# Another way to load and turn the queries and keys of the first head pair

## The chip, the cores and the metric

The kernel runs on one core of a Trainium2 chip. A core has TensorE (matmuls; PE in the profile, PEld for its weight loads), VectorE (DVE), ScalarE (ACT), GpSimd (POOL) and SyncE (SP, which here only issues DMAs), and 16 DMA engines that all queues share. The metric is the device time of one execution in microseconds; the times given are the median of several runs and the time of the one execution that was profiled.

## What is computed

Attention with a threshold, and a feed-forward layer with an ELU behind it:

```python
scores = scale * np.matmul(q, k.transpose(0, 1, 3, 2))      # scale = 1/8
thresh = np.max(scores, axis=-1, keepdims=True) - tau
scores = np.where(scores >= thresh, scores, -1000000000.0)
scores = scores - np.max(scores, axis=-1, keepdims=True)
attn = np.exp(scores)
attn = attn / (np.sum(attn, axis=-1, keepdims=True) + 1e-09)
x = np.matmul(attn, v)             # (8, 8, 576, 64) -> x of (4608, 512)
h = x @ w_in                       # (512, 2048)
g = np.where(h > 0.0, h, np.exp(np.minimum(h, 0.0)) - 1.0)
out = g @ w_out                    # (2048, 512)
```

q, k and v have batch 8, 8 heads, 576 rows and 64 columns, in float32. tau is 0.02, and the kernel reads it at run time.

## The kernel before

**Pairs and steps.** Two heads are worked on together, one on partitions 0 to 63 and one on 64 to 127, so there are 32 pairs, four to a batch entry. The 576 query rows of a pair make five steps: four of 128 rows (i = 0 to 3) and a tail (i = 4) of 64 rows from each head, joined through the tile `qd`. A step consists of the scores of 128 queries against 576 keys for each head (`scores`, L269, matmuls at L283), their maximum on VectorE (`max_of`, L319), the exponential on ScalarE (`exp_of`, L328), the threshold on GpSimd (`bound_of`, L323), the mask with the row sum on VectorE (`mask_of`, L338), the sum and its reciprocal (L347), the normalization on GpSimd (`normalize`, L313), and the turning of the weights on TensorE (`turn_parts`, L365), whose results ScalarE copies out of PSUM (L370). Two steps later follow the products with v (`values`, L479).

**Order of the work.** The first four pairs run in the loop at L780 inside `tc.manual_schedule()`: instructions stand on each engine in the order in which the program names them, and each engine works through its own queue. Later stages (from L870 on) weave the feed-forward layer of earlier batch entries into the attention of later pairs, with an order made by a planner with written-down shifts (`MOVED`); the change doesn't touch them. In the loop, step n works on its scores while the weights of step n-1 are normalized and turned. Idle transposes of the identity (`idle`, L767, and `spare` in `room`, L372) fill TensorE's time: 28 before the first scores, 16 in the first step, then 9 and 11 in each further step of the first pair, and 6 and 8 in later pairs.

**Buffers.** Scores lie in PSUM tiles `sc` from a pool of three (L99). The first step takes two of them. The second step's head 0 takes the third, and its head 1 takes the one that the first step's head 0 frees when its mask has been made. The raw tiles `qm` and `km` (pool `raw`, one buffer for each name) hold a pair's q and k until they are turned.

**How q and k come in.** `load` (L195) fetches q and k of a pair as pieces of 32 numbers: four DMAs for each, one for a head and a half of its 64 columns, each to 32 partitions. The layout is such that VectorE's turn of 32x32 blocks (`prep_q` L219, `prep_k` L228) gives qT and kT, with the 64 columns of each head on partitions. For the first pair SP issues q, then tau, and ACT issues k (L760 to L762); then SP issues v of pair 0, and q, k and v of pair 1. `copy_k` (L240) puts the last 64 keys of head 1 in front of its keys as well, and `copy_q` (L233) fills `qd`; both are on GpSimd. The scores of head 1 read what `copy_k` writes.

**The scale.** In all pairs but the first, GpSimd multiplies qT by `keep` (`scale_q`, L224); `keep` is 1/8 where tau is not negative, and 0 otherwise. In the first pair q is not scaled. There the exponential takes the scale from `keep`, and its bias, the negated maximum, is first multiplied by `keep` on ScalarE (`nb`, L333); the threshold uses `ntau0`, which is `ntau` times 8 (L117). `read_tau` (L111) derives these from tau on VectorE.

Of the kernel before, what the change touches and what calls it, by code (L numbers as in the profile page):

```python
# [10 lines left out]
FP32 = mybir.dt.float32  # L11
U32 = mybir.dt.uint32
I32 = mybir.dt.int32
AF = mybir.ActivationFunctionType
ALU = mybir.AluOpType
# [34 lines left out]
def kernel(  # L50
# [10 lines left out]
    nc = tc.nc  # L61
    PSUM = bass.MemoryType.PSUM
    P = 128
    B, H, S, D = q.shape
# [3 lines left out]
    TAIL = S - MAIN  # L68
    HALF = S // 2
# [7 lines left out]
    SCALE = 1.0 / 8.0  # L77
# [3 lines left out]
    const = ctx.enter_context(tc.tile_pool(name="const", bufs=1))  # L81
    raw = ctx.enter_context(tc.tile_pool(name="raw", bufs=1))
    qkp = ctx.enter_context(tc.tile_pool(name="qkp", bufs=2))
# [9 lines left out]
    wstage = early.enter_context(tc.tile_pool(name="wstage", bufs=2))  # L93
    wpool = [wstage]
    banks = ExitStack()
    psum = {"t": banks.enter_context(tc.tile_pool(name="ps_t", bufs=2, space=PSUM))}
# [4 lines left out]
    ident = wstage.tile([P, P], FP32, name="ident", bufs=1)  # L101
# [4 lines left out]


    tau_sb = const.tile([P, 1], FP32, name="tau_sb")
    pos, keep, far, ntau, ntau0 = (const.tile([P, 1], FP32, name=x) for x in ("pos", "keep", "far", "ntau", "ntau0"))

    def read_tau():  # L111
        nc.vector.tensor_scalar(pos, tau_sb, 0.0, None, ALU.is_ge)
        nc.vector.tensor_scalar(keep, pos, SCALE, None, ALU.mult)
        nc.vector.tensor_scalar(far, pos, -FAR, FAR, ALU.mult, ALU.add)
        nc.vector.tensor_tensor(ntau, tau_sb, far, ALU.max)
        nc.vector.tensor_scalar(ntau, ntau, -1.0, None, ALU.mult)
        nc.vector.tensor_scalar(ntau0, ntau, 1.0 / SCALE, None, ALU.mult)  # L117

    w_in_sb = const.tile([P, KJ, DF], FP32, name="w_in_sb")
    w_out_sb = const.tile([P, NFT, DM], FP32, name="w_out_sb")  # L120
# [4 lines left out]
    qds = [const.tile([P, P], FP32, name=f"qd{i}") for i in range(NQD)]  # L125
# [66 lines left out]
    raws, pairs = {}, {}  # L192


    def load(pr, parts=("qm", "km", "v"), shared=False, queue=nc.sync):  # L195
        b, j = divmod(pr, NPAIR)
        tiles = raws.setdefault(pr, {})
        for name, src in (("qm", q), ("km", k)):
            if name not in parts:
                continue  # L200
            m = tiles[name] = raw.tile([P, S // T, T], FP32, name="qm" if shared else name)
            for i in range(2):
                for d in range(2):
                    r = (2 * i + d) * T
                    queue.dma_start(
                        m[r : r + T],
                        src[b, 2 * j + i].rearrange("(j t) d -> t j d", t=T)[:, :, d * T : (d + 1) * T],
                    )
        if "v" not in parts:
            return  # L210
        vm = tiles["vm"] = raw.tile([P, 2, NC, D], FP32, name="vm", bufs=2)
        vd = tiles["vd"] = vds[pr % NVD]
        for i in range(2):
            vh = v[b, 2 * j + i]
            nc.sync.dma_start(vm[:, i], vh[:MAIN].rearrange("(c p) d -> p c d", p=P))
            r = slice(i * TAIL, (i + 1) * TAIL)
            nc.sync.dma_start(vd[r, r], vh[MAIN:])

    def prep_q(pr):  # L219
        qT = qkp.tile([P, S], FP32, name="qT")  # L220
        nc.vector.transpose(qT, raws[pr]["qm"].rearrange("p j d -> p (j d)"))
        pairs[pr] = [qT, None, qds[pr % NQD]]
# [5 lines left out]
    def prep_k(pr):  # L228
        kT = pairs[pr][1] = qkp.tile([P, TAIL + S], FP32, name="kT")
        nc.vector.transpose(kT[:, TAIL:], raws[pr]["km"].rearrange("p j d -> p (j d)"))  # L230
# [9 lines left out]
    def copy_k(pr):  # L240
        kT = pairs[pr][1]
        nc.gpsimd.tensor_copy(kT[D:, :TAIL], kT[D:, S:])
# [16 lines left out]

    def vectors(pr):  # L260
        st = {x: small.tile([P, 2], FP32, name=x) for x in ("mx", "th", "su", "rs")}
        if not pr:
            st["nb"] = wstage.tile([P, 2], FP32, name="nb", bufs=4)
        step_no[0] += 1
        st["sm"] = totals[:, step_no[0] % 6]
        return st
# [55 lines left out]

    def bound_of(pr, i, h):  # L323
        st = open_steps[pr, i]
        nc.gpsimd.tensor_scalar(st["th"][:, h : h + 1], st["mx"][:, h : h + 1], -1.0, ntau if pr else ntau0, ALU.mult,
                                ALU.add)

    def exp_of(pr, i, h):  # L328
        st = open_steps[pr, i]
        bias = st["mx"][:, h : h + 1]  # L330
        if not pr:
            bias = st["nb"][:, h : h + 1]
            nc.scalar.mul(bias, st["mx"][:, h : h + 1], keep)  # L333
        e = e_slot()
        nc.scalar.activation(e, st[h][:, :, :HALF], AF.Exp, bias=bias, scale=1.0 if pr else keep)
        st[h] = st[h], e

    def mask_of(pr, i, h):  # L338
# [417 lines left out]

    with tc.manual_schedule():
        load(0, ("qm",))  # L760
        nc.sync.dma_start(tau_sb, tau.to_broadcast([P, 1]))
        load(0, ("km",), queue=nc.scalar)  # L762
        load(0, ("v",))
        load(1)


        def idle(n):  # L767
            rt = psum["t"].tile([P, NC, P], FP32, name="rt", tag="rt")
            for _ in range(n):
                transpose(rt[:, 0], ident)  # L770

        idle(28)
        prep_q(0)
        prep_k(0)
        read_tau()
        copy_k(0)
        copy_q(0)
        scores(0, 0, [0, 1])
        out_values = None
        for n in range(per_seq):  # L780
            pr, i = steps[n]
            hs = heads_of(i)
            x = progress[1]
            if n:
                normalize(*steps[n - 1], [0])
                turned = turn_parts(*steps[n - 1])
            max_of(pr, i, 0)
            exp_of(pr, i, 0)
            bound_of(pr, i, 0)

            first_scores = n > 2 and i in (2, NB - 1)
            if n and not first_scores:
                spare.append(6 if pr else 9)
                copies = turned[0]()
            if len(hs) == 2:
                max_of(pr, i, 1)
            if n and len(heads_of(steps[n - 1][1])) == 2:
                normalize(*steps[n - 1], [1])
            if len(hs) == 2:
                exp_of(pr, i, 1)  # L800
                bound_of(pr, i, 1)
            if out_values:
                out_values()
            if n and not first_scores:
                copies()

            if i == NB - 1 and n + 1 < per_seq:
                convert_top(x)
                convert_add(x)
                convert_abs(x)  # L810
                convert_rest(x + 1)
            elif i == 0 and n:
                convert_end(x)
                load_w()
            elif i == 1 and pr:
                convert_sign(x)
                convert_add(x)
            elif i in (2, 3):
                (prep_q if i == 2 else prep_k)(pr + 1)
                if i == 2:  # L820
                    scale_q(pr + 1)
                (copy_q if i == 2 else copy_k)(pr + 1)
            mask_of(pr, i, 0)
            if n and not first_scores:
                spare.append(8 if pr else 11)
                turned[1]()()
            elif not n:
                idle(16)
            if n + 1 < per_seq:
                scores(*steps[n + 1], heads_of(steps[n + 1][1]))  # L830
            if n:
                for part in turned[0 if first_scores else 2 :]:
                    part()()
            if len(hs) == 2:
                mask_of(pr, i, 1)
            reciprocal_of(pr, i, hs)
            out_values = None
            if n > 1 and steps[n - 2][1] in (1, NB - 1):
                out_values = values(steps[n - 2][0], 0 if steps[n - 2][1] == 1 else 1)
            if i == 0 and n:  # L840
                convert_shift(x + 1)
            elif i == 2 and pr:
                convert_end(x)
                load_w()
            if i == 1 and pr:
                convert_abs(x)
            if i == 2 and n + 3 < per_seq:
                convert_rest(progress[1])
            if i in (3, 4):
                load(pr + 2, ("qm",) if i == 3 else ("km",))  # L850
            if i == 3 and pr:
                load(pr + 1, ("v",))
            if n == 0:
                load_w()
                load_w()
        for h in heads_of(steps[per_seq - 1][1]):
            normalize(*steps[per_seq - 1], [h])
# [12 lines left out]
    with tc.manual_schedule():  # L870
# [3 lines left out]
        for n in range(per_seq, SWITCH):  # L874
            pr, i = step = steps[n]
# [167 lines left out]
    with tc.manual_schedule():  # L1043
        after = []
        make_out(1), make_out(0)
        for n in range(SWITCH, MIDDLE):
            pr, i = steps[n]
# [297 lines left out]
        queue = deque()  # L1345
# [213 lines left out]
```

## Time and profile before

| | |
|---|---|
| median of 3 runs | 1319.18 us (1317.34 to 1320.45) |
| profiled execution | 1320.34 us, of which the span of its instructions is 1318.6 us |
| TensorE busy | 1298.9 us (99%) |
| VectorE, ScalarE, GpSimd busy | 1012.1, 559.5 and 805.2 us |
| moved by DMA | 247.76 MB, 188 GB/s in the mean |
| first scores begin (L283) | 8.12 us |
| second step's idle transposes begin | 13.57 us |

Times within the profile are counted from the start of the span. A group or timeline line names the source line, the engine, the operation and "output<-input" with the program's names, then shapes and the count; brackets give how long the engine sat idle before and what released it. A matmul in float32 shows as two instructions. The idle transposes count as busy TensorE, so its 99% is not 99% of useful work.

### The profile page before, as it was taken

What the parts mean: (1) busy time and instruction counts of PE and PEld (TensorE: products, weight loads), DVE (VectorE), ACT (ScalarE), POOL (GpSimd) and SP (SyncE); (2) the same over time, 40 slices, a digit from 0 to 9 for tenths busy, and PEclk for the clock granted to TensorE, in tenths of its full rate; (3) what the DMA queues carried; (4) which work ended last, traced back from release to release, by engine and by line L of the source; (5) the groups of instructions that cost most, each with busy time, mean ns of one, the idle gap of its engine ahead of it and who ended that gap; (6) DMA issues with size and microseconds to landing.
All of it is one profiled execution on the core that took longest, in us unless ns stands there. A gap on an engine that the chain in (4) does not pass through costs nothing.

```text
span 1318.6 us, 22013 instructions
## 1 busy us (share of the span) xinstructions
PE 1298.9 (99%) x6980; PEld 1011.0 (77%) x6980; DVE 1012.1 (77%) x2195; ACT 559.5 (42%) x1219; POOL 805.2 (61%) x1186
## 2 busy tenths in 40 slices
PE   8999999999999999999999999999999999999998
PEld 7666756647778777777878777878777787888886
DVE  6877775988888988898898979897889882545534
ACT  5676664225353444444443535252526250422320
POOL 4657774768657665767475747584768463624533
PEclk9998999999999999999999999999999999999999
DMA  6255452788897989898889888989889775221221
GB/s 120 61 107 161 136 143 57 220 241 241 222 257 221 259 214 245 214 260 232 240 216 256 239 234 224 259 240 245 234 235 258 216 214 185 93 72 60 93 60 32
DMA packets 322595, 247.76 MB, mean 188 GB/s; under 512 B 208688, under 2 KB 284464, under 8 KB 322480
## 3 DMA queue, kind: packets, MB, share of 16 engines
q1 hardware_dynamic: 320112, 246.07, 68.6%
q8 instruction: 55, 0.90, 0.3%
q10 hardware_dynamic: 2368, 0.30, 0.2%
q14 instruction: 60, 0.49, 0.1%
HBM read 161.81 MB, written 84.48 MB: 187 GB/s over the span
## 4 chain that ended last, share of the span: by engine, by line
PE 93%; DVE 3%; DMA 1%; ACT 1%; issue 1%; SPq 1%; POOL 0%; ACTq 0%; DVEq 0%
PE f L1289 29%; PE f L1149 28%; PE sc L541 8%; PE sc L601 7%; PE rt L354 4%; PE sc L283 4%; PE f L652 4%; PE f L692 3%; PE pv L494 3%; PE sc L593 1%; PE sc L588 1%; DMA there<-x 1%; PE pv L489 1%; DVE x L428 1%; SPq L457 0%
## 5 line engine op out<-in xcount | busy, mean ns | idle before, releaser
L317 POOL TENSOR_SCALAR w<-w,rs 128x576 f32<-128x576 f32 x196 | 169.1, 871 | 85.6 <-DVE rs L351 75.5
L548 DVE TENSOR_REDUCE mx<-sc 128x1 f32<-128x576 f32 x207 | 148.3, 750 | 35.3 <-PE sc L541 32.4
L558 ACT ACTIVATE w<-sc,mx 128x576 f32<-128x576 f32 x115 | 83.0, 740 | 114.6 <-DVE mx L548 96.8
L1149 PE MATMUL f<-xt,sw 128*128 128x256 f32 x512 | 123.8, 384 | 0.8 <-ACT xt L611 0.5
L1149 PE MATMUL f<-xt,w_in_sb 128*128 128x256 f32 x512 | 122.3, 381 | 0.3 <-ACT w L1163 0.3
L554 POOL TENSOR_SCALAR th<-mx,ntau 128x2 f32<-128x2 f32 (+1 forms) x115 | 34.3, 298 | 137.8 <-DVE mx L548 137.8
L1149 PEld LDWEIGHTS f<-xt,w_in_sb 128*128 128x128 f32 x512 | 96.1, 190 | 16.0 <-ACT w L1163 3.2
L1149 PEld LDWEIGHTS f<-xt,sw 128*128 128x128 f32 x512 | 93.7, 190 | 18.2 <-ACT xt L611 0.9
L541 PE MATMUL sc<-kT,qT 64*128 64x512 f32 (+4 forms) x736 | 107.5, 423 | 0.0
L1149 PE MATMUL f<-x,w_in_sb 128*128 128x256 f32 x448 | 106.1, 379 | 1.4 <-ACT g L1210 1.4
L1289 PE MATMUL f<-w_out_sb,g 128*128 128x256 f32 x448 | 107.1, 382 | 0.0
L541 PEld LDWEIGHTS sc<-kT,qT 64*128 64x128 f32 x736 | 80.8, 186 | 34.2 <-issue 16.8
L1289 PE MATMUL f<-w_out_sb,s 128*128 128x256 f32 x448 | 107.0, 382 | 0.0
L1289 PE MATMUL f<-t,s 128*128 128x256 f32 x448 | 105.8, 379 | 0.0
L428 DVE STREAM_TRANSPOSE x<-w 128x512 f32<-128x512 f32 (+2 forms) x143 | 96.6, 709 | 10.6 <-POOL w L317 10.3
L562 DVE SCALAR_TENSOR_TENSOR w<-sc,th,w 128x576 f32<-128x576 f32 x115 | 89.8, 811 | 11.4 <-ACT w L558 9.2
L1236 POOL TENSOR_TENSOR s<-g 128x256 f32<-128x256 f32 x104 | 80.4, 779 | 29.4 <-PE f L1289 20.1
L1149 PEld LDWEIGHTS f<-x,w_in_sb 128*128 128x128 f32 x448 | 85.0, 190 | 13.4 <-ACT g L1210 1.8
L1289 PEld LDWEIGHTS f<-w_out_sb,g 128*128 128x128 f32 x448 | 84.1, 190 | 12.9 <-issue 0.7
L1289 PEld LDWEIGHTS f<-t,s 128*128 128x128 f32 x448 | 85.1, 190 | 11.6
L1289 PEld LDWEIGHTS f<-w_out_sb,s 128*128 128x128 f32 x448 | 84.2, 190 | 12.3
L317 POOL TENSOR_SCALAR e<-e,rs 128x576 f32<-128x576 f32 x92 | 68.5, 749 | 35.5 <-DVE rs L351 34.2
(193 smaller groups left out, 2858.7 us busy)
## 6 DMA issues: line engine op xcount, KB each, us to landing
there<-x SPq DMA_DIRECT2D x408, 144.0 KB, 3.7
wTb<-there SPq DMA_DIRECT2D x52, 576.0 KB, 6.5
wTa<-there SPq DMA_DIRECT2D x50, 576.0 KB, 4.9
sw<-win_sums SPq DMA_DIRECT2D x62, 384.0 KB, 4.2
t<-wout_sums SPq DMA_DIRECT2D x45, 512.0 KB, 5.7
qm<-in_q_dram SPq DMA_DIRECT2D x128, 72.0 KB, 4.5
vm<-in_v_dram SPq DMA_DIRECT2D x64, 128.0 KB, 3.2
wst<-in_moe_w_in_dram SPq DMA_DIRECT2D x16, 512.0 KB, 4.4
```

The lines of the kernel that those rows point to most:

```text
L283: nc.tensor.matmul(scs[h][:, a, :HALF], qs[r], kT[r, k0 : k0 + HALF], start=True, stop=True)
L317: nc.gpsimd.tensor_scalar(wv, wv, st["rs"][:, h : h + 1], 1.0, ALU.mult, ALU.mult)
L354: nc.tensor.matmul(dst, src, ident, is_transpose=True, skip_group_check=True)
L428: nc.vector.transpose(x[:, :, c0 : c0 + nc_], src.rearrange("p (c g n) -> p g c n", c=nc_, n=T))
L541: on_banks(nc.tensor.matmul(o, qT[r, i * P : (i + 1) * P], kT[r, k0 : k0 + n], start=True, stop=True, skip_group_check=True), o)
L548: on_banks(nc.vector.tensor_reduce(st["mx"][:, h : h + 1], st["sc", h], axis=AX.XY if i == NC else AX.X, op=ALU.max, negate=True), st["sc" ...
L558: on_banks(nc.scalar.activation(st["e", h], st["sc", h], AF.Exp, bias=st["mx"][:, h : h + 1]), st["sc", h])
L562: on_banks(nc.vector.scalar_tensor_tensor(st["e", h], st["sc", h], st["th"][:, h : h + 1], st["e", h], ALU.is_ge, ALU.mult, accum_out=st[" ...
L601: on_banks(nc.tensor.matmul(o, vm[:, h, c], parts[part][:, g0:g1, h * (NC + 1) + c], start=False, stop=(c == NC - 1), skip_group_check=Tru ...
L1149: nc.tensor.matmul(loc["banks"][place], left[:, j], right[:, j], start=(begins and j == 0), stop=(j == 1), skip_group_check=True)
L1236: engine.tensor_tensor(o, x, y, op)
L1289: nc.tensor.matmul(place(m), lhs, rhs, start=(begins and v == 0), stop=(v == RU - 1), skip_group_check=True)
```

## The change

For the first pair alone, q and k are loaded as rows of 64 numbers. 96 partitions hold six neighbouring rows each, for both heads; SP issues two DMAs for q, and ACT two for k. After 10 idle transposes instead of 28, TensorE turns six tiles of 96 rows for q and six for k into two of the three `sc` tiles in PSUM. VectorE reads q out, multiplied by `keep`, and ScalarE reads k out with a copy; both put every sixth row in its place, so their output steps by six numbers. `read_tau` now stands before these turns. Since the scores of the first pair now come out scaled, `exp_of` and `bound_of` are the same for all pairs: `nb`, its instruction on ScalarE, the scale operand of the exponential and `ntau0` are gone.

```diff
-    pos, keep, far, ntau, ntau0 = (const.tile([P, 1], FP32, name=x) for x in ("pos", "keep", "far", "ntau", "ntau0"))
+    pos, keep, far, ntau = (const.tile([P, 1], FP32, name=x) for x in ("pos", "keep", "far", "ntau"))
...
-        nc.vector.tensor_scalar(ntau0, ntau, 1.0 / SCALE, None, ALU.mult)
...
-        if not pr:
-            st["nb"] = wstage.tile([P, 2], FP32, name="nb", bufs=4)
...
-        nc.gpsimd.tensor_scalar(st["th"][:, h : h + 1], st["mx"][:, h : h + 1], -1.0, ntau if pr else ntau0, ALU.mult,
-                                ALU.add)
+        nc.gpsimd.tensor_scalar(st["th"][:, h : h + 1], st["mx"][:, h : h + 1], -1.0, ntau, ALU.mult, ALU.add)
...
-        bias = st["mx"][:, h : h + 1]
-        if not pr:
-            bias = st["nb"][:, h : h + 1]
-            nc.scalar.mul(bias, st["mx"][:, h : h + 1], keep)
         e = e_slot()
-        nc.scalar.activation(e, st[h][:, :, :HALF], AF.Exp, bias=bias, scale=1.0 if pr else keep)
+        nc.scalar.activation(e, st[h][:, :, :HALF], AF.Exp, bias=st["mx"][:, h : h + 1])
...
+    R = 96
     with tc.manual_schedule():
-        load(0, ("qm",))
+        rows = [wstage.tile([R, S // R, 2, D], FP32, name=x, bufs=1) for x in ("qn", "kn")]
+        for t, src, queue in zip(rows, (q, k), (nc.sync, nc.scalar)):
+            for h in range(2):
+                queue.dma_start(t[:, :, h], src[0, h].rearrange("(p r) d -> p r d", p=R))
         nc.sync.dma_start(tau_sb, tau.to_broadcast([P, 1]))
-        load(0, ("km",), queue=nc.scalar)
         load(0, ("v",))
         load(1)
...
-        idle(28)
-        prep_q(0)
-        prep_k(0)
+        idle(10)
         read_tau()
+        qT, kT = qkp.tile([P, S], FP32, name="qT"), qkp.tile([P, TAIL + S], FP32, name="kT")
+        pairs[0] = [qT, kT, qds[0]]
+        turned = []
+        for t in rows:
+            turned.append(psum["s"].tile([P, 2, 512], FP32, name="sc")[:, :, :HALF].rearrange("p a (r n) -> p a r n", n=R))
+            for x in range(S // R):
+                nc.tensor.matmul(turned[-1][:, x % 2, x // 2], t[:, x].rearrange("p h d -> p (h d)"), ident[:R, :R],
+                                 is_transpose=True, skip_group_check=True)
+        qo, ko = (t.rearrange("d (p r a) -> d a r p", r=S // R // 2, a=2) for t in (qT, kT[:, TAIL:]))
+        nc.vector.tensor_scalar(qo, turned[0], keep, None, ALU.mult)
+        nc.scalar.copy(ko, turned[1])
         copy_k(0)
         copy_q(0)
         scores(0, 0, [0, 1])
```

## The prediction

> **What bounds the kernel now.** I read the shares of busy time and of the chain of waits first, then that chain in order of time over the first 60 us, then windows over single stretches.
>
> ```profile
> PE 1298.9 (99%) x6980; PEld 1011.0 (77%) x6980; DVE 1012.1 (77%) x2195; ACT 559.5 (42%) x1219; POOL 805.2 (61%) x1186
> ...
> PE 93%; DVE 3%; DMA 1%; ACT 1%; issue 1%; SPq 1%; POOL 0%; ACTq 0%; DVEq 0%
> ```
>
> TensorE carries 93% of the chain, and the change leaves the work of pairs 1 to 31 as it is. What it can win or lose lies in the first pair. There the chain reads (start, duration, what):
>
> ```profile
> 2.34 4.41 DMA km<-in_k_dram
> ...
> 7.33 0.73 DVE kT L230
> 8.07 0.05 DVE pos L112
> 8.12 0.01 issue
> 8.12 1.62 PE sc L283 x8
> 9.74 1.90 PE rt L354 x16
> 11.63 0.68 PE sc L283 x2
> 12.31 0.12 issue
> 12.44 1.21 PE sc L283 x6
> 13.64 3.27 PE rt L354 x28
> 16.91 1.17 PE sc L283 x8
> ```
>
> Three places matter: the landing of k at 6.75; the first scores at 8.12; and the pause inside the second step's scores, six of whose eight instructions wait until 12.44. From 13.64 the chain is TensorE alone. That pause is explained by the order of time: the second slot for those scores is freed by the mask of the first step's head 0 (L344), which stands behind this series on ScalarE and VectorE:
>
> ```profile
> 10.19 0.29 ACT L333 ACTIVATE nb<-mx,keep 128x1 f32<-128x1 f32 x1 [6.01 <-DVE mx L321]
> ...
> 10.52 0.83 ACT L335 ACTIVATE e<-sc,nb,keep 128x576 f32<-128x576 f32 x1
> ...
> 11.47 0.82 DVE L344 SCALAR_TENSOR_TENSOR w<-sc,th,e 128x576 f32<-128x576 f32 x1 [0.65 <-ACT e L335]
> ```
>
> From the second step on, the windows of one step each (length, then PE, PEld, DVE, ACT, POOL busy) show TensorE full, and others not:
>
> ```profile
> 13.57:18.01 4.44, 4.44 (x37) 3.71 (x37) 3.44 (x9) 3.10 (x6) 1.95 (x4) 1.00 0.77 215
> 18.01:22.50 4.49, 4.49 (x40) 3.84 (x38) 4.02 (x9) 3.37 (x7) 3.19 (x7) 1.00 0.38 100
> ```
>
> It is full because each step holds 20 idle transposes (9 and 11) of the identity. Their number is not changed.
>
> Two more views, both windows. The first counts the idle transposes (PE column), the second all traffic (last columns: DMA share, GB/s):
>
> ```profile
> 1.45:3.45 2.00, 1.99 (x10) 1.99 (x11) 0.00 (x0) 1.00 0.97 153
> 3.45:5.45 2.00, 2.00 (x11) 2.00 (x11) 0.00 (x0) 1.00 1.48 150
> 9.70:11.50 1.80, 1.80 (x16) 1.70 (x16) 0.00 (x0) 1.00 0.83 133
> ```
>
> ```profile
> 2.25:3.00 0.75, 0.75 (x5) 0.75 (x4) 0.00 (x0) 0.11 (x1) 0.00 (x0) 1.00 1.34 208
> 6.75:7.25 0.50, 0.03 (x1) 0.00 (x0) 0.50 (x1) 0.00 (x0) 0.00 (x0) 1.00 0.96 219
> ```
>
> Idle transposes start every 0.2 us or so up to 5.45, and every 0.11 us (1.80/16) later: TensorE runs at half speed for its first 4 us. The PEclk column shows 1.00 throughout[...].
>
> [...] the gap from 6.8 to 8.1 did not cost the clock. [...] 28 transposes alone brought the full rate. [...] share per GB/s is 0.96/219 with 256-byte packets of v, 1.34/208 with 128-byte ones, a ratio of 0.68. [...] the trace has 832 ns with two (L335, first pair) and 744 ns with one (later pairs): 88 ns.
>
> **The change, part by part.**
>
> *Loading.* The q parts landed at 3.3, 4.3, 5.5 and 6.5 (issue at 0.74 to 2.26, landing 2.6 to 4.3 later), the k parts at 3.6 to 6.75: about 1.07 and 1.04 a part, from a base of 2.25 for q and 2.6 for k. Same bytes, half the packets. If bytes set the pace nothing is won; if packets do, half of 4.3. I take 0.65, near the ratio 0.68: q lands at 2.25 + 0.65 x 4.3 = 5.05, k at 5.3. Bounds: 4.4 and 6.5 for q.
>
> *Issuing.* SP and ACT each issue two DMAs less (0.40 to 0.58 each). On SP, tau, the four v DMAs of pair 0 and the 12 DMAs of pair 1 move up; the first of pair 1 waited until 7.44 for the buffer that L221 read, and no longer does. Pair 1's q and k are read at 19.45 and 23.94: worth nothing, and their earlier packets meet only v. tau landed 0.4 behind the last q (3.67 + 3.3), so I put it at 5.5.
>
> *An added wait.* VectorE now does the tau chain before the q copy; behind that wait stand the q copy and the first maxima. From 8.00 the chain took 0.75 to ntau, so it is over at 6.3. The fifth operation removed (L117, 0.15) lay before an idle stretch: nothing. If tau landed as late as now (6.97), the first scores would come at 8.6, 1.1 later than below.
>
> *Turning.* 12 transposes with 128 columns of weights and 96 moving, against 128 + 128 in an idle one: 224/256 of about 110 ns at full rate, of about 213 ns at half (20 weight loads start from 1.5 to 5.4, the first two together: 18 steps in 3.9): 95 or 187 ns, in all 1.1 or 2.2 us. The 18 idle ones dropped lay in the wait for data; dropping them leaves TensorE idle from 3.6 to 5.1. I take it that the clock comes back at about 5.6 as now [...]: 2.5 transposes at half rate and 9.5 at full end at 6.5, the last result is there at 6.7.
>
> *Reading out.* ScalarE copies 128x512 in 0.589 and 128x256 in 0.373, so 576 columns in 0.64. The output steps by 24 bytes, which no row shows; L156, which reads and writes every second word, takes 0.69 for 512 columns, 17% over a copy. Bounds 0.64 and, doubled, 1.28; I take 0.70. VectorE's q copy, priced as its maximum over the same PSUM shape (0.75), runs from 6.35 to 7.1 and is hidden behind the k copy, 6.75 to 7.45. Without that cover it costs what it exceeds 7.45. GpSimd's copy of k's tail follows as now. First scores at 7.5 against 8.12: **-0.6**. Two DVE turns (0.78, 0.73) are gone; they are in the 8.12.
>
> *The table load* (1.28, now at 2.89) may slide behind the k copy: it then ends 0.7 before the first exponential wants it (scores + 1.28 + 0.76). Nothing.
>
> *No bias instruction.* In the first step 10.52 - 10.19 = 0.33 and 0.09 of the exponential go, on the series that frees the slot at 12.31: **-0.42**. TensorE's 16 idle transposes end at 11.64, 0.8 before 12.44, so they don't take this back. In the other four steps the same is off the path, since TensorE is full there.
>
> *Sum:* -0.6 - 0.42 = -1.0 at 13.64, carried by TensorE to the end. Profiled 1320.34 (span 1318.6 and 1.74 around it) becomes 1319.3; the median of the runs lies 1.16 lower, 1319.18, and becomes 1318.2.
>
> **Rivals.**
>
> [...] All 12 transposes at half rate: last result at 7.55, first scores at 8.3 (+0.2), the first 0.65 us of them at half rate (+0.3), less 0.42: +0.1, **1319.3**. [...] Against: the gap of 1.3 us that the trace shows harmless.
>
> *Slower: half rate through the first step.* Place: the eight scores and the 16 idle transposes behind them. The scores take 1.0 longer; the 16 idle ones, half at 213 ns, now end last, and the second scores end 1.2 later: **1320.4**. It decides once the clock is not back before the first scores, at 8.3. If in addition the rows land only at 6.5, +2.2.
>
> *The bias instruction counts in every step.* Were ScalarE and VectorE the bound in the first pair, 4 more times 0.42: -2.7, **1316.5**. Against it stand the full PE windows.
>
> *The change does nothing for loading,* bytes setting the pace: q at 6.5, full rate, first scores at 8.7, less 0.42: +0.15, **1319.3**. For it: equal steps of 1.05 per 144 KB. Against: 0.68.
>
> **How the numbers follow.** Forecast 0.45; later clock 0.20; nothing for loading 0.12; half rate through the step 0.14; every step 0.09. About 0.2% (2.6 us) is what a measurement of this kernel can tell from no change. Runs spread by 1.5 us to each side. Faster by over that: the every-step rival and a part of the spread, 0.10. Slower: the worse end of the half-rate rival, 0.06. Range: from the every-step rival to +1.9, between half rate and late rows together: 1316.5 to 1321.1.
>
> **What would show it.** Landings of the rows near 5.05; starts of the transposes 95 ns apart in their later part (187 ns: a rival); first scores at 7.5; no pause longer than now in the second scores, which end at 12.6; later steps of 4.45 to 4.5 as now. It is wrong if rows land past 6, if the 16 idle transposes are over 0.2 us apart, or if steps of the first pair shrink below 4.4.

## The result, and the profile after

The kernel after takes **1323.3 us** in the median of 13 runs (1320.2 to 1324.97), the kernel before 1319.18 in as many beside it: ratio 1.0028 [1.0018, 1.0037]. It is slower by 0.28%; the medians lie 4.1 us apart. Forecast were 1318.2 and at most 1321.1. The profiled execution took 1324.2 us with a span of 1322.4, against 1320.34 and 1318.6: 3.8 us more.

Shares of busy time, and shares of the chain of waits, of the kernel after:

```profile
PE 1300.5 (98%) x6974; PEld 1013.2 (77%) x6974; DVE 1011.7 (77%) x2193; ACT 557.9 (42%) x1211; POOL 804.3 (61%) x1186
...
PE 92%; DVE 3%; DMA 2%; ACT 1%; POOL 1%; issue 1%; SPq 0%; DVEq 0%; ACTq 0%; POOLq 0%
```

TensorE is busy for 1.6 us longer with six instructions fewer, so some of them were slower. The chain of waits of the kernel after, in order of time (start, duration, what):

```profile
1.52 4.49 DMA qn<-in_q_dram
...
6.14 2.17 PE sc L774 x12
...
8.34 1.18 ACT kT L778
...
9.56 2.67 PE sc L280 x8
12.22 3.57 PE rt L346 x16
15.79 1.17 PE sc L280 x8
16.97 3.21 PE rt L346 x28
```

Read beside the chain of before: the first scores begin at 9.56 instead of 8.12 (+1.44). They take 2.67 instead of 1.62 (+1.05), and the 16 idle transposes behind them 3.57 instead of 1.90 (+1.67). The second scores run through in 1.17, where before they stood in two parts from 11.63 to 13.64 (-0.84). Together that is +3.32, and the second step's idle transposes begin at 16.97 instead of 13.64, which is +3.33 (both by the chain; the timeline has them begin 0.07 earlier). From there on the order is as before, and the same instruction comes between 3.1 and 4.3 us later than before up to the end. So 3.3 of the 3.8 us arise in the first 17 us. Another 0.7 is added between 80 and 95 us; no run here separates its cause.

The windows of the kernel after show the rate (length, then PE, PEld, DVE, ACT, POOL busy with counts, PEclk, DMA share, GB/s):

```profile
3.45:6.10 2.65, 0.41 (x2) 0.00 (x1) 0.00 (x0) 0.00 (x0) 0.00 (x0) 1.00 1.13 214
...
12.20:14.00 1.80, 1.80 (x10) 1.80 (x10) 1.57 (x3) 1.33 (x2) 0.53 (x2) 1.00 0.60 131
14.00:15.70 1.70, 1.70 (x9) 1.43 (x7) 1.42 (x6) 0.08 (x1) 0.10 (x1) 1.00 0.94 255
...
16.96:19.00 2.04, 2.04 (x20) 2.04 (x20) 1.72 (x3) 1.14 (x2) 1.15 (x3) 1.00 0.07 26
```

After 10 idle transposes TensorE stands still for over 2 us (2.24, first line). The 16 idle transposes start some 0.2 us apart up to 15.7 (1.80/10 and 1.70/9), as at the very start, and 0.1 us apart only later (2.04/20, last line). TensorE works at half rate for its first 14 us instead of 4, and PEclk says 1.00 all the while. The trace's record of the granted clock has its first entry at 5.70 us before and at 15.63 after; nothing is recorded ahead of it, and the column reads that as full speed.

Two lines of the timeline of the kernel after answer to the pause in the second scores:

```profile
13.54 0.82 DVE L336 SCALAR_TENSOR_TENSOR w<-sc,th,e 128x576 f32<-128x576 f32 x1 [0.23 <-ACT e L327]
...
15.72 1.24 PE L280 MATMUL sc<-kT,qT 64*128 64x288 f32 x8
```

The mask that frees the slot is over at about 14.3, and the second scores start at 15.72, behind the idle transposes. The pause is gone, but TensorE's own work has taken its place.

### The profile page after: what moved, and what is told of

It is laid out like the page before. It is cut to its first block, busy times and chain, and to the rows that moved or that the text cites. A ratio compares the mean times of both kernels' runs of the same rounds, so it can differ in the third digit from the quotient of the medians.

```text
span 1322.4 us, 21988 instructions
## 1 busy us (share of the span) xinstructions
PE 1300.5 (98%) x6974; PEld 1013.2 (77%) x6974; DVE 1011.7 (77%) x2193; ACT 557.9 (42%) x1211; POOL 804.3 (61%) x1186
## 4 chain that ended last, share of the span: by engine, by line
PE 92%; DVE 3%; DMA 2%; ACT 1%; POOL 1%; issue 1%; SPq 0%; DVEq 0%; ACTq 0%; POOLq 0%
PE f L1292 29%; PE f L1152 27%; PE sc L533 8%; PE sc L593 7%; PE rt L346 4%; PE sc L280 4%; PE f L644 4%; PE f L684 3%; PE pv L486 2%; PE sc L585 1%; DMA there<-x 1%; PE sc L580 1%; PE pv L481 1%; DVE x L420 1%; DMA wTb<-there 0%
```

## The experiments

**Theory.** The dropped idle transposes cost the full rate of the first step, some 3 us; reading out with a 24-byte step costs another half, and the rows of q land late for a reason of their own. **Rivals:** the loss lies in loading and reading out, and the rate only accompanies it; or the first step's series on ScalarE and VectorE bounds, and the rate of idle work doesn't matter.

### The idle transposes, back in and taken out

In the kernel after, 24 instead of 10:

```diff
-        idle(10)
+        idle(24)
```

> The changed kernel with 24 idle transposes in place of 10, so that TensorE is busy until the rows land at about 6.0 us. Theory (half clock): in the changed kernel TensorE runs at half rate until 15.6 us because it idles from 3.9 to 6.1; with the gap filled it is at full rate from about 5.6, the turns take 1.0 us instead of 2.0, the eight scores 1.6 instead of 2.7, the 16 idle transposes 1.8 instead of 3.6: the second scores end near 13.7, and the time is about 3.3 us below the changed kernel, near 1319.5. Rival (reading out and late rows): the clock costs little beside the 1.2 us copies, the time stays within 1 us of the changed kernel, near 1322.5.

Measured: 1320.76 us, ratio to before 1.0008 [1.0000, 1.0016]. Its chain in order of time:

```profile
1.46 4.45 PE rt L346 x24
...
6.04 1.19 PE sc L774 x12
...
7.26 1.17 ACT kT L778
...
8.47 1.62 PE sc L280 x8
10.09 1.90 PE rt L346 x16
11.99 1.60 PE sc L280 x8
13.58 3.21 PE rt L346 x28
```

One number brings back 2.5 us (3.3 were expected), so the rival on which the rate only accompanies the loss falls for the larger part. The 12 turns take 1.19 instead of 2.17, the scores 1.62, the 16 idle ones 1.90. The second step is where it was before the change (13.58 against 13.64), so nothing is won either.

The counterpart, in the kernel before, with all else as it was:

```diff
-        idle(28)
+        idle(10)
```

> The kernel before with 10 idle transposes in place of 28, nothing else. Theory (half clock): TensorE idles from 3.9 to 8.1 and then runs the first scores and the 16 idle transposes at half rate; first scores still begin at 8.1, the second scores end about 2.3 us later than before: near 1321.5. Rival (clock is not the cause): within 0.5 us of the kernel before, 1319.2.

Measured: 1321.34 us, ratio 1.0013 [1.0007, 1.0020]. In its chain the first scores take 2.67 instead of 1.62, the 16 idle ones 3.17 instead of 1.90, and the second step's begin at 15.07 instead of 13.64:

```profile
8.06 2.67 PE sc L283 x8
10.73 3.17 PE rt L354 x16
13.90 1.17 PE sc L283 x8
15.07 3.21 PE rt L354 x28
```

Rows, turns on VectorE and bias are untouched, so the rate alone makes the old kernel slower, too. The rival on which the rate of idle work doesn't matter falls.

Fewer idle transposes within the first step of the kernel after, since at half rate they seemed to end last:

```diff
-                idle(16)
+                idle(4)
```

> The changed kernel with 4 idle transposes in the first step in place of 16. Theory (at half rate the 16 idle transposes end last in the first step): the second scores begin when the first mask is made, near 14.4 in place of 15.7, but still at half rate, so they end 0.5 to 1.3 us earlier, if the clock does not come back later for it: near 0.8 us below the changed kernel. Rival (the mask ends last there, as in the kernel before): no difference.

Measured: 1323.62 us, ratio 1.0033 [1.0022, 1.0045]: no gain, a miss. The four take 1.04 and the second scores begin at 13.07, but their last six instructions wait until 14.28 for the mask, all are at half rate (3.50 for eight), and the next idle transposes begin at 16.57. The record of the clock has its first entry at 17.87, where with all 16 it was at 15.63. So with fewer of the idle transposes that hold up the scores, the rate came back 2.24 us later.

### Rows and reading out

Each partition holds rows 96 apart instead of six neighbours. Then both copies write without a step:

```diff
-                queue.dma_start(t[:, :, h], src[0, h].rearrange("(p r) d -> p r d", p=R))
+                queue.dma_start(t[:, :, h], src[0, h].rearrange("(r p) d -> p r d", p=R))
...
-                nc.tensor.matmul(turned[-1][:, x % 2, x // 2], t[:, x].rearrange("p h d -> p (h d)"), ident[:R, :R],
+                nc.tensor.matmul(turned[-1][:, x // 3, x % 3], t[:, x].rearrange("p h d -> p (h d)"), ident[:R, :R],
...
-        qo, ko = (t.rearrange("d (p r a) -> d a r p", r=S // R // 2, a=2) for t in (qT, kT[:, TAIL:]))
+        qo, ko = (t.rearrange("d (a r p) -> d a r p", r=S // R // 2, a=2) for t in (qT, kT[:, TAIL:]))
```

> The changed kernel with each partition holding rows 96 apart instead of six neighbours, so that both copies out of PSUM write without a step; packets stay at 256 bytes. Theory (half clock): the k copy falls from 1.17 to 0.64 us, the first scores come 0.5 earlier, half rate stays to about 15.6: 0.5 us below the changed kernel, near 1322.8. Rival (reading out is the main cost): over 1.5 us below it, under 1321.8.

Measured: 1322.05 us, ratio 1.0013 [1.0006, 1.0020]: 1.25 less than after, more than the half microsecond expected from the copies alone. Its chain:

```profile
1.20 3.94 DMA qn<-in_q_dram
...
5.28 2.17 PE sc L774 x12
...
7.46 0.65 ACT kT L778
...
8.16 2.67 PE sc L280 x8
```

The k copy takes 0.65 instead of 1.18, and the last row of q is there at 5.14 instead of 6.01. The second is seen in the issues. Of the tile `qn` in the kernel after, the issue line (ns, least, median, most), then the time from issue to landing:

```profile
L756 SPq DMA_DIRECT2D qn<-in_q_dram x2: 734/800/867, 0.7 to 1.5; - x2
...
DMA to landing us min/median/max: 3.9/4.2/4.5
```

The same in the kernel with rows 96 apart:

```profile
L756 SPq DMA_DIRECT2D qn<-in_q_dram x2: 403/448/492, 0.7 to 1.2; - x2
...
DMA to landing us min/median/max: 3.2/3.6/3.9
```

The six neighbouring rows of a partition are 1536 bytes in one piece at the source and six pieces of 256 at the destination. In this layout a DMA of q took 0.80 us to issue instead of 0.45 (one of k, on ACT, 0.68 instead of 0.52), and in the traces the first 256-byte packet of q starts at 2.76 us instead of 1.81. Not all of the rows gain, however. The DMAs of k have the same two shapes, but their first packet starts at 2.23 instead of 2.14, and their last row lands at 5.52 in the kernel after and at 5.86 with rows 96 apart. So q and k change places in the order of landing, and the last row of all comes only 0.15 us earlier. q is turned first, so the turns gain from q. What in the layout makes q start late was not shown; turning k first was not tried.

To tell the step from the order, the third layout keeps the neighbouring rows; the copies write in order and read PSUM with a step of 96 numbers:

```diff
-        qo, ko = (t.rearrange("d (p r a) -> d a r p", r=S // R // 2, a=2) for t in (qT, kT[:, TAIL:]))
+        qo, ko = (t.rearrange("d (p r a) -> d p r a", r=S // R // 2, a=2) for t in (qT, kT[:, TAIL:]))
+        turned = [t.rearrange("d a r p -> d p r a") for t in turned]
```

> The changed kernel with the copies out of PSUM in the order of the output: they write without a step and read PSUM with a step of 96 numbers. Theory (a write step of 24 bytes doubles the copy): the k copy takes 0.65 us, the q copy 0.75. Rival (any step on either side doubles it): 1.17 and 1.22 as in the changed kernel.

One run: 1323.16 us, and in its timeline:

```profile
7.25 0.82 DVE L778 TENSOR_SCALAR qT<-sc,keep 128x576 f32<-128x576 f32 x1 [0.31 <-PE sc L774]
...
8.20 0.64 ACT L779 COPY kT<-sc 128x576 f32<-128x576 f32 x1 [4.79 <-PE sc L774]
```

0.64 and 0.82, against 1.17 and 1.22: the step in what is written nearly doubled the k copy and made the q copy half as long again. The step in what is read cost nothing to be seen: with rows 96 apart, where neither side has one, the two take 0.64 and 0.81. A step of 24 bytes in what is written cost the k copy 0.53 us for 576 numbers.

Rows 96 apart and 18 idle transposes together, in the kernel after:

```diff
-        idle(10)
+        idle(18)
```

> The changed kernel with rows 96 apart (copies without a step, rows at about 5.1 us) and 18 idle transposes, which keep TensorE busy until then. Theory (half clock, plus the copies and the late start of the rows): full rate from about 5.6, first scores at 7.5, second scores end at 12.6, which is what the prediction had forecast: 1.0 us below the kernel before. Rival (the clock does not come back this early [...]): half rate to 9 or later, not below the kernel before.

Measured: 1318.81 us, ratio 0.9996 [0.9987, 1.0004]. Level with before, where 1.0 below had been expected, and below after by 4.5. Its chain no longer goes through rows and k copy but through tau (landed at 6.11), its five small operations and the q copy, to scores at 7.79. TensorE waits 1.18 us for these, and behind that wait it loses the full rate again: the record of the clock has full rate from 4.52 and half rate from 7.93 to 11.35, and the scores and the idle transposes are slow once more:

```profile
7.79 2.37 PE sc L280 x8
10.16 2.48 PE rt L346 x16
```

### The bias instruction

In the kernel before, `ntau0`, `nb` and the scale of the exponential are taken out; this leaves the scaling of the first pair's scores out.

```diff
-            bias = st["nb"][:, h : h + 1]
-            nc.scalar.mul(bias, st["mx"][:, h : h + 1], keep)
...
-        nc.scalar.activation(e, st[h][:, :, :HALF], AF.Exp, bias=bias, scale=1.0 if pr else keep)
+        nc.scalar.activation(e, st[h][:, :, :HALF], AF.Exp, bias=bias)
```

> The kernel before without the bias instruction, the scale operand of the exponential and the second threshold; it leaves the scaling of the first pair's scores out. Theory: only the first step's share counts, since TensorE is full in the later steps: the second scores end 0.4 us earlier, the time is 0.4 below before, near 1318.8. Rival (counts in every step of the first pair): 2.1 below, near 1317.1.

Measured: 1320.11 us beside 1320.16, ratio 1.0000 [0.9992, 1.0008]. In its chain the second scores run without a pause, and the second step's idle transposes begin at 13.22 instead of 13.64: the 0.42 is won at its place. The end doesn't show it: the runs of one kernel lie too far apart.

### A second place where the rate falls, at 101 us

Runs of one kernel lie some 4 us apart. The kernel before shows where from, far from the change. Its timeline:

```profile
103.51 2.57 PE L283 MATMUL sc<-kT,qT 64*128 64x288 f32 x8 [2.18 <-DVE w L344]
```

and one of its windows there:

```profile
107.00:110.00 3.00, 3.00 (x12) 1.23 (x12) 2.71 (x9) 1.28 (x2) 3.00 (x5) 0.50 0.83 294
```

Where the second loop (from L870) begins, TensorE waits 2.18 us for a mask, and from 104.69 the granted clock is 0.50 for 6.83 us. In the profiled executions this period is absent, 3.41 or 6.83 us long, with the same code around it. The runs fall into groups to match: of the 59 runs of the kernel before in one series (the one with 24 idle transposes), 5 have a mean granted clock of 1.000 and a median of 1317.32 us, 13 have 0.998 and 1318.81, and 36 have 0.996 or 0.997 and about 1320.5. So 18 idle transposes were put into that wait, in the kernel before:

```diff
+            if n == per_seq:
+                idle(18)
```

> The kernel before with 18 idle transposes put into the first step of the second loop, where TensorE waits from 101.3 to 103.5 us for a mask. Theory (that wait makes the clock fall to half for one or two windows near 105 us in most runs, which costs 1.5 to 3 us): the runs crowd near 1317.4, 2.5 us below the kernel before. Rival (the half rate there has another cause): no difference, 1320.2.

Measured: **1317.15 us** (1316.92 to 1318.46 in 21 runs), ratio 0.9982 [0.9976, 0.9989]. The same window now reads:

```profile
107.00:110.00 3.00, 2.75 (x22) 1.43 (x18) 2.86 (x9) 2.64 (x7) 3.00 (x5) 1.00 0.93 309
```

The clock stays at 1.00, and the runs crowd within 0.5 us but for the profiled one. They take what the kernel before takes when the period is absent: its 24 runs with a mean clock of 1.000 have medians of 1317.10 to 1317.43 us in the four series of measurements. This is a better kernel than both, and a better scale, but not a perfect one: this kernel and those below come from different series, and by these medians a difference of 0.3 us between two series says nothing. The remaining kernels carry these two lines as well; their further edits are those shown above.

The kernel after with them:

> The changed kernel with the 18 idle transposes at 101 us that kept the clock up there in the kernel before. Theory (the loss is made in the first 17 us, by the clock, the copies and the late rows; the half rate near 105 us only adds noise to both): the runs lie 3 to 3.5 us above the kernel before with the same 18 transposes (1317.15), near 1320.4. Rival (a part of the loss comes from more half rate near 105 us in the changed kernel): under 2.5 above it, below 1319.7.

1321.02 us, ratio to before 1.0011 [1.0004, 1.0017]; 3.87 above the kernel before with them. The change's loss is thus no matter of the place at 101 us. Of this 3.87, with 24 idle transposes at the start instead of 10:

> The same, with 24 idle transposes at the start in place of 10. Theory: the clock is worth 2.5 to 3 us of the loss; copies with a step (0.5), late rows and the longer path are left, less 0.4 for the bias: near 1317.4. Rival (clock secondary): above 1319.

1318.11 us, ratio 0.9992 [0.9984, 1.0000]: 2.91 of it is gone, 0.96 is left (0.25 had been expected). The filling has a price of its own. In this profile the record of the clock has full rate from 7.22, not from 4.82 as in the first run with 24; the idle transposes last until 6.84 and not 5.91, and the turns, whose q rows are there at 5.94, wait for them. With rows 96 apart, still with 10:

> The changed kernel with 18 idle transposes at 101 us and rows 96 apart, 10 idle ones at the start. Theory: rows 0.8 earlier and copies 0.5 shorter at low clock, 1 to 1.4 below the changed kernel with the 18 (1321.0), near 1319.8. Rival (earlier rows only put the first step further into the half rate): within 0.5 of it.

1319.91 us, ratio 1.0003 [0.9994, 1.0011]: 1.11 gone, as expected (1.38, when each is set against the clock-1.000 runs of the kernel before in its own series). With both, rows 96 apart and 18 idle transposes:

> 18 idle transposes at the start, rows 96 apart, and the 18 at 101 us. Theory: 0.4 to 1.0 below the kernel before with the 18 transposes at 101 us (1317.15) if the clock stays up through the first step, near 1316.5; where the clock falls again while TensorE waits for the copies, about 1 above that.

1317.27 us, ratio 0.9984 [0.9978, 0.9990]: 0.12 above the kernel before with the fill, where 0.4 to 1.0 below had been expected. That is the same, within the intervals; the change in its best form here is worth nothing over the old way that the medians show, and both beat the two original kernels. In the profile it is ahead where it should be: its second step's idle transposes begin at 12.86 instead of 13.50, and 0.4 of these 0.64 us are left at 95 us. Its chain goes through tau again (landed at 6.10, scores at 7.78), so tau was moved ahead of the rows on SP, with six idle transposes behind the turns:

```diff
+        nc.sync.dma_start(tau_sb, tau.to_broadcast([P, 1]))
         rows = [wstage.tile([R, S // R, 2, D], FP32, name=x, bufs=1) for x in ("qn", "kn")]
...
-        nc.sync.dma_start(tau_sb, tau.to_broadcast([P, 1]))
...
+        idle(6)
```

> The same, with tau's DMA ahead of the q rows and 6 idle transposes between the turns and the first scores. Theory (in the version with rows 96 apart tau lands last and the q copy waits for its chain): q copy from 6.5 in place of 6.9, first scores near 7.5, and the clock does not fall in between: 1316.0 to 1316.5. Rival (tau first delays the rows by what it saves): no difference to the version without it.

1319.36 us, ratio 1.0002 [0.9994, 1.0010]: worse by 2.1, where a gain of about 1 had been expected. The last row of q lands at 6.79 instead of 5.25; scores begin at 8.84. Its second DMA is issued 0.45 us later (1.65 instead of 1.20), and then takes 5.1 us instead of 3.9 to 4.2. With tau's transfer of four bytes to a partition put first, the rows of q behind it landed 1.54 us later. Of the 2.1, 1.1 are there when the second step's idle transposes begin (13.95); the rest was not traced.

Two more, on the kernel before with the fill. With 10 instead of 28 idle transposes:

> The kernel before with 18 idle transposes at 101 us and 10 in place of 28 at the start. Theory: half rate through the first scores and the 16 idle transposes, no turns on TensorE: 1.5 to 2 us above 1317.15, near 1318.9. Rival (the clock costs the same 2.9 without the turns): near 1320.

1318.98 us, ratio 0.9999 [0.9991, 1.0007]: 1.83 more, as expected (1.55 against the clock-1.000 runs of its own series). Without the bias instructions (the first pair's scaling left out again):

> The kernel before with 18 idle transposes at 101 us and without the bias instruction, the scale operand and the second threshold; it leaves the scaling of the first pair's scores out. Theory: only the first step's share counts, 0.4 below 1317.15, near 1316.7. Rival (every step): 1315.0. Second rival (nothing): 1317.15.

1317.09 us, ratio 0.9981 [0.9974, 0.9988]: 0.06 less than with them. In the two profiles the second step's idle transposes begin at 13.09 and 13.50, and TensorE's instructions stay 0.4 to 0.6 apart up to 95 us and 0.4 apart up to 590 us. There the kernel with the bias, whose profiled run was its slowest, falls back by another 1.4 us. So the gain is made, and nothing takes it back up to there. That the two medians hide it may be due to their series: beside the 8 clock-1.000 runs of the kernel before in its own series (median 1317.43) this kernel is 0.34 faster, the kernel with the fill beside 3 in its series (1317.10) no faster. These runs were picked out afterwards, so this points to about 0.4 at the end, too, and doesn't prove it.

## Why the prediction was wrong

**The step that failed** is in the part on turning: "I take it that the clock comes back at about 5.6 as now". It came back at 15.6 (15.63 in the record). It was assumed, and the rival named for it, half rate through the first step, is what happened, at the place that it named. Keeping TensorE busy at the start brings back 2.9 of 3.87 us. The mistake was to carry a finding across: that the gap from 6.8 to 8.1 did not *lose* the full rate was taken to say that a similar gap does not *prevent* it. Even the finding was no rule: with 18 idle transposes and rows 96 apart, a gap of 1.18 us did lose the rate (half from 7.93 to 11.35). The clock records say more. Within a trace their entries lie whole multiples of 3.413 us apart (before, 98.99 us from 5.70 to 104.69, which is 29 of them; after, 92.16 us from 15.63 to 107.79, which is 27). Counted back from the first entry in such lengths, TensorE had worked through nearly all of the last stretch, idle for at most 0.35 us of it, while stretches with more idling brought nothing (after: 0.76 us between 8.80 and 12.21; rows 96 apart, entry at 12.10: 0.72 us, from 7.43 to 8.15, in the stretch from 5.27 to 8.69, which was 79% busy). By this count a stretch with the 1.5 us of idling that was forecast (3.6 to 5.1) would not have been enough. Where the limit lies is open: with rows 96 apart and the fill, a stretch with 0.17 us of idling (8.23 to 11.64) brought nothing either. The stretches are an estimate from the spacing of the entries; no trace records them.

**The rival's size** was 1320.4, and the end of the range, 1321.1, came from it. It counted only half of the 16 idle transposes at 213 ns; all were (+1.67 instead of about 0.8), and the first scores began at 9.56, not 8.3.

**Loading.** For q, forecast 5.05, landed 6.01; for k, 5.3 and 5.52. The pace was right: the two q DMAs land 1.38 us apart (4.63 and 6.01), the two k DMAs 1.56 (3.96 and 5.52); against two old parts, 2 x 1.07 and 2 x 1.04, that is 0.65 and 0.75. The start of q was wrong. "0.40 to 0.58 each" was carried over to a DMA of another shape, which takes 0.73 and 0.87 on SP, and q's packets begin at 2.76, about 1 us later than with rows 96 apart. Bounds of 4.4 and 6.5 held it.

**Added wait.** tau was over at 7.1, not 6.3, and hid behind the k copy nevertheless, by luck: the k copy was later still (q is ready at 8.60, k at 9.51). It became the bound as soon as rows, copies and rate were mended (scores at 7.79 and 7.78). The step was right about what comes last next.

**Turning.** 2.17 us for 12 against 1.1 to 2.2: the estimate by columns, 187 ns each at half rate and 95 at full, was near (2.17/12 = 181; with 24 idle transposes 1.19/12 = 99), the choice of rate was not.

**Reading out.** k copy 1.17 instead of 0.70, within the bounds, near the doubled end; "17% over a copy" was taken from a row with an 8-byte step. q copy 1.22 instead of 0.75, hidden as said. The first scores moved from the forecast 7.5 to 9.56: 0.96 from loading, 0.65 from turning, 0.47 from the copy, 2.1 in all, so +1.44 against before in place of -0.6.

**Table load, issuing, GpSimd's copy:** nothing, as forecast; the table load ran from 2.15 to 3.43.

**No bias instruction.** The mechanism is right: the exponential, which took 832 ns with bias and scale both from tiles, takes 744 in later pairs with the bias alone; the pause goes, and where the rate is full 0.41 or 0.42 is seen at 13 us. In the kernel after it is worth nothing, because the idle transposes end 1.4 us behind the mask. That "TensorE's 16 idle transposes end at 11.64, 0.8 before 12.44" held only at full rate.

**Later steps.** 4.38 and 4.48 (16.97, 21.35, 25.83), against 4.44 and 4.49 before; the rival of the bias in every step, 0.42 in each, is out, and so is that of loading at the old pace. Of the signs of being wrong that it named, two came clearly: rows past 6 (6.01), and the 16 idle transposes over 0.2 us apart (3.57/16 = 0.22). The third, steps below 4.4, came by 0.02 in one step.

## What to carry to other kernels

Work that fills a wait at the start may be what raises TensorE's rate: here 10 idle transposes instead of 24 moved the full rate from 4.82 to 15.63 us and cost 2.5 us. Before dropping it, ask when the rate comes back if a gap opens there, and don't take a gap that kept the rate (1.3 us here) as leave for one that precedes it (2.3 us); read the rate from the spacing of equal instructions (0.2 us here at half rate, 0.1 at full), not from a column that may have no entry yet and then says 1.00. Price a copy and a DMA with the strides that they will have: here writing with a 24-byte step nearly doubled the k copy, and with six neighbouring rows to a partition the last row of q landed 0.7 to 0.9 us later than with rows 96 apart.

## What the runs showed of the hardware

Both kernels lost rate where the second loop begins, behind one wait of 2.18 us in the middle of steady work, and not in every execution: in the two profiles the granted clock is 0.50 for 6.83 us, from 104.69 before and from 107.79 after. All nine profiled executions without the fill have this wait. Counted in the stretches of 3.413 us that were estimated from the clock entries of each trace, it fell into one stretch, at least 1.93 us of it, in six of them, and 6.83 us at half rate followed. Split over two stretches as 1.07 and 1.08 it was followed by 3.41 us (two executions), split as 1.47 and 0.68 by none (one). So as far as nine traces show, what followed went with where the wait lay against these stretches; that they are the cause was not shown. A wait of 2.18 us was followed by half rate in eight of nine executions here, and filling it with 18 transposes was worth 0.18% [0.11%, 0.24%]: 2.4 us, over twice the 1.0 that was forecast for the change.
